# Second layer of groups 1 to 8 as seven half-size products, with fp16 sums of h and wo, and max terms on ScalarE

## The chip, the cores and the metric

The kernel runs on one core of one Trainium2 chip. The metric is the device time of one execution in microseconds (us); lower is better. Each time below is the median of the runs of one kernel, with the lowest and the highest beside it. A profiled execution is shown next to the times; its span is a little shorter than the device time (319.2 us of span for 321.17 us of device time in the kernel before).

## The reference

Linear attention with phi(x) = elu(x) + 1 on 8 batches, 8 heads, 576 positions and head size 64, followed by a SwiGLU feed-forward block on the 4608 tokens (d_model 512, d_ff 1536). Inputs and outputs are fp32.

```python
q_p, k_p = phi(q), phi(k)                       # phi(x) = max(x, 0) + min(exp(x), 1)
kv  = einsum('bhsd,bhse->bhde', k_p, v)
z   = sum(k_p, axis=2)
x   = einsum('bhsd,bhde->bhse', q_p, kv) / (einsum('bhsd,bhd->bhs', q_p, z)[..., None] + 1e-06)
x   = x.transpose(0, 2, 1, 3).reshape(4608, 512)
out = (silu(x @ w_gate) * (x @ w_val)) @ w_out  # 512 -> 1536 -> 512
```

## The kernel before

The kernel works in fp16 with fp32 accumulation. The 4608 tokens are nine groups g = 0 to 8 of 512. In each group, layer 1 has twelve blocks `fb`. A block is four gate matmuls and four value matmuls of 512 columns; ScalarE then applies silu, and VectorE multiplies it with the value half into `hT`. Layer 2 has four token tiles of twelve 512-column matmuls each, and one eviction per tile (times 1/SC) into `osb`, which goes out by DMA. While TensorE works on group g, the other engines prepare the attention of the next batches: phi of k and q, the denominators (`prod`, reduce, reciprocal, scale), a transpose by DMA, and on TensorE the small matmuls `mm2` (they give `xT`, the input of the next group) and `mm1` (k times v; called through `joint`).

```python
def phi(src, e, dst, b, lp):                     # e holds exp(src), from ScalarE
    s = slice(2 * lp, 2 * lp + 2)
    nc.vector.tensor_scalar(out=e[:, s, :], in0=e[:, s, :], scalar1=1.0, scalar2=None, op0=ALU.min)
    for l in range(2 * lp, 2 * lp + 2):
        nc.vector.scalar_tensor_tensor(              # max(src, 0) + e, 576 columns
            out=dst[b % 2][:, :, D * l:D * l + D],
            in0=src[b % 2][:, l, :].rearrange("p (j d) -> p j d", d=D), scalar=0.0,
            in1=e[:, l, :].rearrange("p (j d) -> p j d", d=D), op0=ALU.max, op1=ALU.add)

def l1_gate(g, fb):
    (pg, pv), s = l1_banks(g, fb), sil[fb % 2]
    nc.scalar.activation(out=s[:, :], in_=pg[:, :], func=AF.Silu, bias=0.0, scale=1.0)
    nc.vector.scalar_tensor_tensor(out=hT[g % 2][:, fb, :], in0=pv[:, :], scalar=SC, in1=s[:, :],
                                   op0=ALU.mult, op1=ALU.mult)

def l2(g, t, f0=0, f1=FB):
    pso[(g, t)] = (pV[0], pG[0], pV[1], pG[1])[t]
    for fb in range(f0, f1):
        nc.tensor.matmul(out=pso[(g, t)][:, :], lhsT=hT[g % 2][:, fb, P * t:P * t + P], rhs=wo[:, fb, :],
                         start=(fb == 0), stop=(fb == FB - 1))
# ... l2_out: one eviction of 512 columns, then two output transfers on SyncE's queue
# ... l2_last: the last tile of group 8 in two halves of 256 columns, its outputs on two queues

def prep(b):                                     # phi of batch b, slotted after the four tiles
    return at(4, [(0, lambda: exp_k(b, 0)), (0, lambda: exp_k(b, 1)), (1, lambda: exp_q(b, 0)),
                  (1, lambda: exp_q(b, 1)), (1, lambda: phi_k(b, 0)), (2, lambda: phi_k(b, 1)),
                  (3, lambda: nc.scalar.preload_act_table_set("silu_and_others")), (3, lambda: phi_q(b, 0))])

for g in range(1, NG):
    # ... sl: side work after each block; w: leftovers of it for layer 2 (in group 1: two denominator steps)
    for fb in range(FB):
        l1(g, fb)
        for f in sl[fb]:
            f()
        # ... loads of later batches, issued by GpSimd
    for t in range(4):
        if t == 3 and b1 < NG:
            mm2(b1, pV[2], "AVAV")
            if b2 < B:
                joint(b2)
        # ... l2_last for the last tile of the last group
        l2(g, t)
        for f in w[t] + pre[t]:
            f()
        l2_out(g, t, A if t in (1, 3) else V)
```

In these traces VectorE and ScalarE take their work in program order (below, VectorE stands idle for 1.19 us with later work ready, and silu on ScalarE starts only after max terms of 1.18 and 1.16 us), so where a call stands in this loop is where it stands in their queues.

## Time and profile before

| | before |
|---|---|
| time, median of 3 runs (lowest to highest) | 321.0 us (320.78 to 321.17) |
| span of the profiled run | 319.2 us |
| TensorE, VectorE, ScalarE, GpSimd busy | 98%, 66%, 54%, 10% |
| layer 2 of a steady group, from its first matmul to the next group's layer 1 | 11.66 us |
| layer 1 of a steady group | 20.93 us |
| from the modelled end of the last matmul to the end of the span | 4.6 us |

From the page of the kernel before: busy time and share of each engine with its instruction count, the granted TensorE clock over 40 equal slices in tenths, and the chain of work that ended last by engine.

```profile
PE 311.8 (98%) x2191; PEld 148.5 (47%) x2191; DVE 211.3 (66%) x393; ACT 171.3 (54%) x246; POOL 31.9 (10%) x47
...
PEclk9999999999999999999999999999999999999999
...
PE 89%; DMA 4%; DVE 2%; POOL 2%; ACT 2%; issue 1%; SPq 0%; POOLq 0%; ACTq 0%
```

TensorE (PE) is busy 98% of the span at a mean granted clock of 0.998, and the chain that ended last lies on it for 89%. So a microsecond of TensorE is a microsecond of the kernel, and other engines' time counts only where TensorE waits for it.

From the timeline of TensorE in the kernel before, in layer 2 of group 3. The columns are start, duration, engine, line, operation, output and inputs, shape and count.

```profile
142.69 2.75 PE L303 MATMUL pV<-wo,hT 128*128 128x512 f16 x12
145.28 2.75 PE L303 MATMUL pG<-wo,hT 128*128 128x512 f16 x12
```

From the same view, at the end of group 8:

```profile
311.79 1.47 PE L324 MATMUL pG<-wo,hT 128*128 128x256 f16 x12
313.10 1.47 PE L324 MATMUL pX<-wo,hT 128*128 128x256 f16 x12
```

The starts are 2.59 us apart for 12 matmuls of 512 columns, or 216 ns each, and 1.31 us for 12 of 256, or 109 ns each. The last tile of this kernel thus already shows the pace of the half-size products.

### The profile page before, as it was taken

How to read it: one execution, taken by the hardware profiler on the slowest of the kernel's cores; microseconds unless marked ns; L12 is line 12 of the kernel's file. 1: busy time of each engine (PE TensorE's matmuls, PEld its weight loads, DVE VectorE, ACT ScalarE, POOL GpSimd, SP SyncE). 2: the span in 40 equal slices, each digit the busy share in tenths (PEclk: the TensorE clock that was granted, in tenths of full speed). 3: DMA queues.
4: the chain of work that ended last, by engine and by line, in shares of the span. 5: the costliest groups of instructions: out<-in, count | busy, mean ns of one | idle time of the engine just before them, and what ended most of it. 6: DMA issues, size and time to landing. Idle time of an engine off the chain costs nothing.

```text
span 319.2 us, 5573 instructions
## 1 busy us (share of the span) xinstructions
PE 311.8 (98%) x2191; PEld 148.5 (47%) x2191; DVE 211.3 (66%) x393; ACT 171.3 (54%) x246; POOL 31.9 (10%) x47
## 2 busy tenths in 40 slices
PE   8999999999999999999999999999999999999994
PEld 6644453444444454445444454445444444444443
DVE  3747749878978877887888787877883344134411
ACT  3869969748563765467536754585431333133310
POOL 8535310010020001000010000000000000000000
PEclk9999999999999999999999999999999999999999
DMA  7999999994579147924792430233022400140014
GB/s 101 194 200 200 204 207 208 260 210 85 118 140 166 33 93 139 154 46 90 142 149 50 87 74 0 49 71 89 2 49 59 101 0 0 35 99 0 2 35 97
DMA packets 40986, 32.21 MB, mean 101 GB/s; under 512 B 16256, under 2 KB 36480, under 8 KB 40960
## 3 DMA queue, kind: packets, MB, share of 16 engines
q0 software_dynamic: 20640, 18.88, 38.0%
q1 hardware_dynamic: 20160, 12.85, 18.4%
q8 instruction: 17, 0.28, 0.4%
q10 hardware_dynamic: 160, 0.13, 0.2%
q14 instruction: 9, 0.07, 0.1%
HBM read 37.75 MB, written 9.44 MB: 148 GB/s over the span
## 4 chain that ended last, share of the span: by engine, by line
PE 89%; DMA 4%; DVE 2%; POOL 2%; ACT 2%; issue 1%; SPq 0%; POOLq 0%; ACTq 0%
PE pV L282 28%; PE pG L282 27%; PE pV L303 14%; PE pG L303 13%; DMA wv<-in_moe_w_val_dram 3%; PE pX L282 2%; PE pX L254 1%; DVE osb L313 1%; DMA out_dram<-osb 1%; PE pV L172 1%; DVE xT L435 1%; ACT rr L432 1%; ACT rr L429 1%; POOL k L99 0%; POOL v L99 0%
## 5 line engine op out<-in xcount | busy, mean ns | idle before, releaser
L288 DVE SCALAR_TENSOR_TENSOR hT<-pV,sil 128x512 f16<-128x512 f32 x105 | 72.2, 691 | 57.0 <-PE pV L282 53.2
L282 PE MATMUL pV<-xT,wv 128*128 128x512 f16 x420 | 108.1, 379 | 0.3 <-DMA wv<-in_moe_w_val_dram 0.3
L282 PE MATMUL pG<-xT,wg 128*128 128x512 f16 x408 | 105.1, 379 | 0.7 <-DVE osb L313 0.6
L287 ACT ACTIVATE sil<-pG 128x512 f16<-128x512 f32 x102 | 60.6, 597 | 78.4 <-PE pG L282 51.2
L282 PEld LDWEIGHTS <-wv 128*128 128x128 f16 x432 | 42.2, 98 | 51.6 <-DMA wv<-in_moe_w_val_dram 1.1
L282 PEld LDWEIGHTS <-wg 128*128 128x128 f16 x432 | 41.8, 98 | 51.0 <-issue 1.5
L303 PEld LDWEIGHTS <-hT 128*128 128x128 f16 x420 | 39.8, 98 | 47.6 <-issue 1.2
L303 PE MATMUL pV<-wo,hT 128*128 128x512 f16 x216 | 50.2, 379 | 0.0
L303 PE MATMUL pG<-wo,hT 128*128 128x512 f16 x204 | 47.6, 380 | 0.0
L313 DVE TENSOR_SCALAR osb<-pV 128x512 f32<-128x512 f32 x18 | 12.4, 690 | 25.3 <-PE pV L303 25.3
L311 ACT ACTIVATE osb<-pG 128x512 f32<-128x512 f32 x15 | 8.8, 589 | 19.9 <-PE pG L303 19.8
L127 DVE SCALAR_TENSOR_TENSOR kp<-k,ek 128x576 f16<-128x576 f16 x24 | 17.1, 755 | 0.4
L127 DVE SCALAR_TENSOR_TENSOR qp<-q,eq 128x576 f16<-128x576 f16 x24 | 17.1, 755 | 0.4
L235 DVE TENSOR_TENSOR qp<-qp,rden 128x768 f16<-128x768 f16 x18 | 17.1, 949 | 0.0
L222 DVE TENSOR_REDUCE den<-prod 128x12 f32<-128x768 f16 x18 | 17.0, 943 | 0.0
L269 ACT ACTIVATE xT<-pX 128x512 f16<-128x512 f32 (+1 forms) x14 | 7.4, 579 | 16.7 <-PE pX L254 9.3
L121 ACT ACTIVATE ek<-k 128x1152 f16<-128x1152 f16 x14 | 15.6, 1154 | 0.1
L121 ACT ACTIVATE eq<-q 128x1152 f16<-128x1152 f16 x14 | 15.4, 1148 | 0.0
L147 ACT ACTIVATE vm<-v 128x1152 f16<-128x1152 f16 x12 | 14.1, 1175 | 0.0
L96 POOL DMA_DIRECT2D k<-in_k_dram x7 | 5.4, 766 | 76.8 <-DVE kp L127 53.8
L365 PE MATMUL pX<-sil,ones 128*128 128x256 f16 x51 | 8.9, 350 | 1.3 <-DVE sil L356 1.3
L217 DVE TENSOR_TENSOR prod<-qp,zbc 128x768 f16<-128x768 f16 x18 | 9.3, 516 | 1.4 <-ACT zbc L208 1.3
(105 smaller groups left out, 218.1 us busy)
## 6 DMA issues: line engine op xcount, KB each, us to landing
out_dram<-osb SPq DMA_DIRECT2D x70, 128.0 KB, 2.4
k<-in_k_dram POOLq DMA_DIRECT2D x7, 576.0 KB, 13.2
q<-in_q_dram POOLq DMA_DIRECT2D x7, 576.0 KB, 7.5
v<-in_v_dram POOLq DMA_DIRECT2D x7, 576.0 KB, 9.6
wg<-in_moe_w_gate_dram POOLq DMA_DIRECT2D x6, 256.0 KB, 11.7
wv<-in_moe_w_val_dram POOLq DMA_DIRECT2D x6, 256.0 KB, 11.9
wo<-in_moe_w_out_dram POOLq DMA_DIRECT2D x3, 512.0 KB, 15.8
k<-in_k_dram POOLq DMA_DIRECT2D x2, 288.0 KB, 5.7
```

Source lines behind the costliest of these rows:

```text
L121: nc.scalar.activation(out=e[:, s, :], in_=src[b % 2][:, s, :], func=AF.Exp, bias=0.0, scale=1.0)
L127: nc.vector.scalar_tensor_tensor(out=dst[b % 2][:, :, D * l:D * l + D], in0=src[b % 2][:, l, :].rearrange("p (j d) -> p j d", d=D), scalar ...
L147: nc.scalar.activation(out=vm[b % 2][:, :, s, 0:D].rearrange("p j l d -> p l j d"), in_=v16[b % 2][:, s, :].rearrange("p l (j d) -> p l j ...
L217: nc.vector.tensor_tensor(out=prod[:, 0:j1 - j0, :], in0=qp[b % 2][:, j0:j1, :], in1=zbc[:, :].unsqueeze(1).to_broadcast([P, j1 - j0, HL * ...
L222: nc.vector.tensor_reduce(out=den[:, HL * j0:HL * j1], in_=prod[:, 0:j1 - j0, :].rearrange("p j (l d) -> p (j l) d", d=D), axis=AX.X, op=A ...
L235: nc.vector.tensor_tensor(out=qv, in0=qv, in1=rden[:, HL * j0:HL * j1].unsqueeze(2).to_broadcast([P, HL * (j1 - j0), D]), op=ALU.mult)
L282: nc.tensor.matmul(out=ps[:, :], lhsT=src[:, i, P * fb:P * fb + P], rhs=xT[i][g % 2][:, :], start=(i == 0), stop=(i == 3))
L287: nc.scalar.activation(out=s[:, :], in_=pg[:, :], func=AF.Silu, bias=0.0, scale=1.0)
L288: nc.vector.scalar_tensor_tensor(out=hT[g % 2][:, fb, :], in0=pv[:, :], scalar=SC, in1=s[:, :], op0=ALU.mult, op1=ALU.mult)
L303: nc.tensor.matmul(out=pso[(g, t)][:, :], lhsT=hT[g % 2][:, fb, P * t:P * t + P], rhs=wo[:, fb, :], start=(fb == 0), stop=(fb == FB - 1))
L313: nc.vector.tensor_scalar(out=o[:, :], in0=ps[:, :], scalar1=1.0 / SC, scalar2=None, op0=ALU.mult)
L365: nc.tensor.matmul(out=dst[:, 0:256], lhsT=ones[:, :], rhs=sil[0][:, 0:256], start=True, stop=True)
```

## The change

The intent is to do less on TensorE. Split h into two halves by token and two halves by d_ff (even and odd blocks), and wo into two halves by d_ff and two by column. The Winograd form of Strassen's scheme then needs seven products of half-size blocks in place of eight: 84 matmuls of 256 columns per group in place of 48 of 512. It needs four sums of the blocks of h in every group (on VectorE), four sums of the blocks of wo once (on GpSimd, in group 0), and combinations of the products. Most of the combinations are made by letting products accumulate in the same bank; ScalarE keeps copies of the partial results (`part`), and VectorE adds them in the eviction. To make room on VectorE, the max term of phi moves to ScalarE for batches 3 to 7. The diff, cut to its core (with the lambdas of `prep` and the index expressions shortened):

```diff
+def relu(src, dst, b, lp):                       # max(src, 0), 1152 columns
+    s = slice(2 * lp, 2 * lp + 2)
+    nc.scalar.activation(out=dst[b % 2][...], in_=src[b % 2][...], func=AF.Relu, bias=0.0, scale=1.0)
+def phi_sum(e, dst, b, lp):
+    nc.vector.tensor_scalar(out=e[:, s, :], in0=e[:, s, :], scalar1=1.0, scalar2=None, op0=ALU.min)
+    nc.vector.tensor_tensor(out=d, in0=d, in1=e[:, s, :]..., op=ALU.add)
 def phi_k(b, lp):
-    phi(k16, ek, kp, b, lp)
+    phi_sum(ek, kp, b, lp) if b > 2 else phi(k16, ek, kp, b, lp)
 # ... phi_q likewise

+def h_sum(g, m, f0, f1):                         # four sums or differences of blocks of hT
+    nc.vector.tensor_tensor(out=hs[:, m, f0:f1, :], in0=a, in1=b, op=op)
+def w_sum(m, f0, f1):                            # four differences of blocks of wo
+    nc.gpsimd.tensor_tensor(out=ws[:, m, f0:f1, :], in0=a, in1=b, op=ALU.subtract)
+def prd(g, n, tt):                               # product n for token half-tile tt: 6 matmuls of 256
+    for f in range(HF):
+        nc.tensor.matmul(out=(z if n in (2, 3, 5) else x)[:, 0:HD], lhsT=left(f), rhs=right(f),
+                         start=(f == 0 and n in (1, 2, 5)), stop=(f == HF - 1), ...)
+def keep(tt, i, from_x):                         # ScalarE: partial result to SBUF
+    nc.scalar.activation(out=part[:, 2 * i + tt, :], in_=(x if from_x else z)[:, 0:HD], func=AF.Copy, ...)
+def fin(tt, th, ch, i, from_x):                  # VectorE: bank * 1/SC + part -> osb
+    nc.vector.scalar_tensor_tensor(out=osb[...], in0=..., scalar=1.0 / SC, in1=part[:, 2 * i + tt, :], ...)
+def put(g, tt, th, c0=0, c1=DM, engs=(nc.sync, nc.sync)):
+    # ... two output transfers
+def l2_steps(g):
+    return [(p[1][0],), (p[1][1], k1[0]), (p[2][0], k1[1]), (p[2][1], c11[0]), (p[6][0], c11[1]), (p[6][1], k2[0]),
+            (p[5][0], k2[1]), (p[5][1], k5[0]), (p[7][0], k5[1]), (p[7][1], c22[0]), (p[3][0], c22[1]),
+            (p[3][1], lambda: c12(0)), (p[4][0], lambda: c12(1)), (p[4][1], lambda: fin_21(g, 0)),
+            (lambda: fin_21(g, 1),)]

 def prep(b):
-    return at(4, [(0, exp_k(b, 0)), (0, exp_k(b, 1)), (1, exp_q(b, 0)), (1, exp_q(b, 1)), (1, phi_k(b, 0)),
-                  (2, phi_k(b, 1)), (3, preload of silu), (3, phi_q(b, 0))])
+    return at(16, [(2, exp_k(b, 0)), (6, exp_k(b, 1)), (6, phi_k(b, 0)), (8, phi_k(b, 1)), (9, exp_q(b, 0)),
+                   (10, exp_q(b, 1)), (14, preload of silu), (14, phi_q(b, 0))])

 # group 0, layer 2, before each third of it:
+        for m in range(4):
+            w_sum(m, 2 * i, 2 * i + 2)
 # groups 1 to 8:
+            for lp in range(2):
+                sl[4 + lp].append(lambda lp=lp: relu_k(b2, lp))
+                sl[6 + lp].append(lambda lp=lp: relu_q(b2, lp))
+        for m in range(4):
+            sl[(8, 8, 9, 10)[m]].append(lambda m=m: h_sum(g, m, 0, 4))
+            sl[11].append(lambda m=m: h_sum(g, m, 4, 6))
+        for t in range(3):
+            pre[3 * t + 2][:0] = w[t]            # leftovers of the denominator
+        for (i, step) in enumerate(l2_steps(g)):
+            for f in step: f()
+            if i == (11 if g == 1 else 8) and b1 < NG:
+                mm2(b1, (pV[1], pG[1], pV[0], pG[0]), "AVAV")
+            if i == (9 if g == 1 else 10) and b2 < B:
+                joint(b2)
+            for f in pre[i]: f()
```

Products are numbered as in the code. Products 1 and 2 read `hT` itself, 5, 6 and 7 read a sum of h and a sum of wo, 3 reads a sum of h, and 4 a sum of wo. Product 5 starts in the bank that product 2 used, so it waits for the first eviction.

More of the change, by code (lines that the diff above doesn't have):

```diff
@@ L74 @@
     osb = two([P, DM], FP32, "osb", 4)
+    hs = sb.tile([P, 4, FB // 2, U * C // 2], FP16, name="hs")
+    ws = sb.tile([P, 4, FB // 2, DM // 2], FP16, name="ws")
+    part = sb.tile([P, 6, DM // 2], FP32, name="part")
     wg = sb.tile([P, 4, DF], FP16, name="wg")
@@ L84 @@
     pX = [pp.tile([P, 512], FP32, name=f"pX_{i}") for i in range(3)]
-    turn = [0]
-    def bank():
-        turn[0] += 1
-        return pX[turn[0] % 3]
     def heads(src, b):
@@ L130, in phi, with relu_k, relu_q @@
                 in1=e[:, l, :].rearrange("p (j d) -> p j d", d=D), op0=ALU.max, op1=ALU.add)
+    def relu(src, dst, b, lp):
+        s = slice(2 * lp, 2 * lp + 2)
+        nc.scalar.activation(out=dst[b % 2][:, :, P * lp:P * lp + P].rearrange("p j (s d) -> p s j d", d=D),
+                             in_=src[b % 2][:, s, :].rearrange("p s (j d) -> p s j d", d=D),
+                             func=AF.Relu, bias=0.0, scale=1.0)
+    def relu_k(b, lp):
+        relu(k16, kp, b, lp)
+    def relu_q(b, lp):
+        relu(q16, qp, b, lp)
+    def phi_sum(e, dst, b, lp):
+        s = slice(2 * lp, 2 * lp + 2)
+        nc.vector.tensor_scalar(out=e[:, s, :], in0=e[:, s, :], scalar1=1.0, scalar2=None, op0=ALU.min)
+        d = dst[b % 2][:, :, P * lp:P * lp + P].rearrange("p j (s d) -> p s j d", d=D)
+        nc.vector.tensor_tensor(out=d, in0=d, in1=e[:, s, :].rearrange("p s (j d) -> p s j d", d=D), op=ALU.add)
     def exp_k(b, lp):
@@ L138, in phi_k @@
     def phi_k(b, lp):
-        phi(k16, ek, kp, b, lp)
+        phi_sum(ek, kp, b, lp) if b > 2 else phi(k16, ek, kp, b, lp)
     def phi_q(b, lp):
-        phi(q16, eq, qp, b, lp)
+        phi_sum(eq, qp, b, lp) if b > 2 else phi(q16, eq, qp, b, lp)
     def vcast(b, lp):
@@ L159, in mm1 @@
         if lp == 0:
-            kvb[b] = ((pV[2], pX[0]), (pX[2], pV[2]), (pX[0], pX[1]), (pV[0], pG[0]))[min(b, 3)]
+            kvb[b] = ((pV[2], pX[0]), (pX[2], pV[2]), (pX[0], pX[1]), (pV[1], pG[1]))[min(b, 3)]
         for j in range(J):
@@ L200, in zb @@
     def zb(b):
-        zps[b] = bank()
+        zps[b] = pX[0]
         nc.tensor.matmul(out=zps[b][:, :], lhsT=ones[:, :], rhs=zd[:, :, :].rearrange("p i c -> p (i c)"),
@@ L255, in corners, with mm2 @@
                                      rhs=qT[b % 2][rows, j0:j1, lp, C * hh:C * hh + C], start=True, stop=True)
-    def mm2(g, spare, engs):
-        ps = [bank(), bank(), bank(), spare]
+    def mm2(g, ps, engs):
         us = units(g)
@@ L317, in l2_out @@
                               in_=o[C * e:C * e + C, :])
-    def l2_last(g, t):
-        banks = (pG[1], pX[0])
-        for h in range(2):
-            for fb in range(FB):
-                nc.tensor.matmul(out=banks[h][:, 0:256], lhsT=hT[g % 2][:, fb, P * t:P * t + P],
-                                 rhs=wo[:, fb, 256 * h:256 * h + 256], start=(fb == 0), stop=(fb == FB - 1))
-        for h in range(2):
-            for e in range(2):
-                o = osb[ot[0] % 4]
-                ot[0] += 1
-                rows = slice(C * e, C * e + C)
-                if e == 0:
-                    nc.vector.tensor_scalar(out=o[rows, 0:256], in0=banks[h][rows, 0:256], scalar1=1.0 / SC,
-                                            scalar2=None, op0=ALU.mult)
-                else:
-                    nc.scalar.activation(out=o[rows, 0:256], in_=banks[h][rows, 0:256], func=AF.Copy, bias=0.0,
-                                         scale=1.0 / SC)
-                b, j = units(g)[2 * t + e]
-                (nc.sync, nc.scalar)[e].dma_start(
-                    out=out[S * b:S * b + S, 256 * h:256 * h + 256].rearrange("(c j) f -> j c f", j=J)[j],
-                    in_=o[rows, 0:256])
@@ new lines, with h_blk, w_blk @@
+    HF, HT, HD = FB // 2, U * C // 2, DM // 2
+    def h_blk(g, kh, th, f0, f1):
+        return hT[g % 2][:, 2 * f0 + kh:2 * f1 - 1 + kh:2, HT * th:HT * th + HT]
+    def w_blk(kh, ch, f0, f1):
+        return wo[:, 2 * f0 + kh:2 * f1 - 1 + kh:2, HD * ch:HD * ch + HD]
+    def h_sum(g, m, f0, f1):
+        o = hs[:, m, f0:f1, :]
+        (a, b, op) = ((h_blk(g, 0, 1, f0, f1), h_blk(g, 1, 1, f0, f1), ALU.add),
+                      (hs[:, 0, f0:f1, :], h_blk(g, 0, 0, f0, f1), ALU.subtract),
+                      (h_blk(g, 0, 0, f0, f1), h_blk(g, 0, 1, f0, f1), ALU.subtract),
+                      (h_blk(g, 1, 0, f0, f1), hs[:, 1, f0:f1, :], ALU.subtract))[m]
+        nc.vector.tensor_tensor(out=o, in0=a, in1=b, op=op)
@@ new lines, in w_sum, with l2_banks, left, right @@
+    def w_sum(m, f0, f1):
+        o = ws[:, m, f0:f1, :]
+        (a, b) = ((w_blk(0, 1, f0, f1), w_blk(0, 0, f0, f1)), (w_blk(1, 1, f0, f1), ws[:, 0, f0:f1, :]),
+                  (w_blk(1, 1, f0, f1), w_blk(0, 1, f0, f1)), (w_blk(1, 0, f0, f1), ws[:, 1, f0:f1, :]))[m]
+        nc.gpsimd.tensor_tensor(out=o, in0=a, in1=b, op=ALU.subtract)
+    def l2_banks(tt):
+        return (pX[0], pX[1])[tt], (pX[2], pV[2])[tt]
+    def prd(g, n, tt):
+        (x, z) = l2_banks(tt)
+        th = P * tt
+        def left(f):
+            h = hT[g % 2]
+            return {1: h[:, 2 * f, th:th + P], 2: h[:, 2 * f + 1, th:th + P], 3: hs[:, 3, f, th:th + P],
+                    4: h[:, 2 * f + 1, HT + th:HT + th + P], 5: hs[:, 0, f, th:th + P], 6: hs[:, 1, f, th:th + P],
+                    7: hs[:, 2, f, th:th + P]}[n]
+        def right(f):
+            return {1: wo[:, 2 * f, 0:HD], 2: wo[:, 2 * f + 1, 0:HD], 3: wo[:, 2 * f + 1, HD:DM], 4: ws[:, 3, f, :],
+                    5: ws[:, 0, f, :], 6: ws[:, 1, f, :], 7: ws[:, 2, f, :]}[n]
+        for f in range(HF):
+            nc.tensor.matmul(out=(z if n in (2, 3, 5) else x)[:, 0:HD], lhsT=left(f), rhs=right(f),
+                             start=(f == 0 and n in (1, 2, 5)), stop=(f == HF - 1), skip_group_check=True)
@@ new lines, in keep @@
+    def keep(tt, i, from_x):
+        (x, z) = l2_banks(tt)
+        nc.scalar.activation(out=part[:, 2 * i + tt, :], in_=(x if from_x else z)[:, 0:HD], func=AF.Copy, bias=0.0,
+                             scale=1.0 / SC)
+    def fin(tt, th, ch, i, from_x):
+        (x, z) = l2_banks(tt)
+        nc.vector.scalar_tensor_tensor(out=osb[2 * th + tt][:, HD * ch:HD * ch + HD],
+                                       in0=(x if from_x else z)[:, 0:HD], scalar=1.0 / SC, in1=part[:, 2 * i + tt, :],
+                                       op0=ALU.mult, op1=ALU.add)
@@ new lines, in put, with fin_21 @@
+    def put(g, tt, th, c0=0, c1=DM, engs=(nc.sync, nc.sync)):
+        for e in range(2):
+            b, j = units(g)[2 * (2 * th + tt) + e]
+            engs[e].dma_start(out=out[S * b:S * b + S, c0:c1].rearrange("(c j) f -> j c f", j=J)[j],
+                              in_=osb[2 * th + tt][C * e:C * e + C, c0:c1])
+    def fin_21(g, tt):
+        x = l2_banks(tt)[0]
+        o = osb[2 + tt]
+        if g < NG - 1 or tt == 0:
+            nc.scalar.activation(out=o[:, 0:HD], in_=x[:, 0:HD], func=AF.Copy, bias=0.0, scale=1.0 / SC)
+            put(g, tt, 1)
+            return
+        put(g, tt, 1, HD, DM)
+        nc.vector.tensor_scalar(out=o[0:C, 0:HD], in0=x[0:C, 0:HD], scalar1=1.0 / SC, scalar2=None, op0=ALU.mult)
+        nc.scalar.activation(out=o[C:P, 0:HD], in_=x[C:P, 0:HD], func=AF.Copy, bias=0.0, scale=1.0 / SC)
+        put(g, tt, 1, 0, HD, (nc.sync, nc.scalar))
@@ new lines, in l2_steps, with c12 @@
+    def l2_steps(g):
+        p = [[(lambda n=n, tt=tt: prd(g, n, tt)) for tt in range(2)] for n in range(8)]
+        k1, k2, k5 = [[(lambda i=i, tt=tt, x=x: keep(tt, i, x)) for tt in range(2)]
+                      for (i, x) in ((0, True), (1, True), (2, False))]
+        c11 = [lambda tt=tt: fin(tt, 0, 0, 0, False) for tt in range(2)]
+        c22 = [lambda tt=tt: fin(tt, 1, 1, 2, True) for tt in range(2)]
+        def c12(tt):
+            fin(tt, 0, 1, 1, False)
+            put(g, tt, 0)
+        return [(p[1][0],), (p[1][1], k1[0]), (p[2][0], k1[1]), (p[2][1], c11[0]), (p[6][0], c11[1]), (p[6][1], k2[0]),
+                (p[5][0], k2[1]), (p[5][1], k5[0]), (p[7][0], k5[1]), (p[7][1], c22[0]), (p[3][0], c22[1]),
+                (p[3][1], lambda: c12(0)), (p[4][0], lambda: c12(1)), (p[4][1], lambda: fin_21(g, 0)),
+                (lambda: fin_21(g, 1),)]
@@ L601, in prep @@
     def prep(b):
-        return at(4, [(0, lambda: exp_k(b, 0)), (0, lambda: exp_k(b, 1)), (1, lambda: exp_q(b, 0)),
-                      (1, lambda: exp_q(b, 1)), (1, lambda: phi_k(b, 0)), (2, lambda: phi_k(b, 1)),
-                      (3, lambda: nc.scalar.preload_act_table_set("silu_and_others")), (3, lambda: phi_q(b, 0))])
+        return at(16, [(2, lambda: exp_k(b, 0)), (6, lambda: exp_k(b, 1)), (6, lambda: phi_k(b, 0)),
+                       (8, lambda: phi_k(b, 1)), (9, lambda: exp_q(b, 0)), (10, lambda: exp_q(b, 1)),
+                       (14, lambda: nc.scalar.preload_act_table_set("silu_and_others")), (14, lambda: phi_q(b, 0))])
     def ld_b(b):
@@ L657 @@
         sl, w = [[] for _ in range(FB)], [[] for _ in range(4)]
-        pre = [[] for _ in range(4)]
+        pre = [[] for _ in range(16)]
         if b1 < B:
@@ L662 @@
             pre = prep(b2)
-            sl[8].append(lambda: vcast(b2, 0))
-            sl[9].append(lambda: vcast(b2, 1))
+            for lp in range(2):
+                sl[4 + lp].append(lambda lp=lp: relu_k(b2, lp))
+                sl[6 + lp].append(lambda lp=lp: relu_q(b2, lp))
+                sl[8 + lp].append(lambda lp=lp: vcast(b2, lp))
+        for m in range(4):
+            sl[(8, 8, 9, 10)[m]].append(lambda m=m: h_sum(g, m, 0, 4))
+            sl[11].append(lambda m=m: h_sum(g, m, 4, 6))
         for fb in range(FB):
@@ L672 @@
                 ld_b(3)
-        for t in range(4):
-            if t == 3 and b1 < NG:
-                mm2(b1, pV[2], "AVAV")
-                if b2 < B:
-                    joint(b2)
-            if g == NG - 1 and t == 3:
-                l2_last(g, t)
-                continue
-            l2(g, t)
-            for f in w[t] + pre[t]:
-                f()
-            l2_out(g, t, A if t in (1, 3) else V)
+        for t in range(3):
+            pre[3 * t + 2][:0] = w[t]
+        for (i, step) in enumerate(l2_steps(g)):
+            for f in step:
+                f()
+            if i == (11 if g == 1 else 8) and b1 < NG:
+                mm2(b1, (pV[1], pG[1], pV[0], pG[0]), "AVAV")
+            if i == (9 if g == 1 else 10) and b2 < B:
+                joint(b2)
+            for f in pre[i]:
+                f()
 _INS = ['q', 'k', 'v', 'moe_w_gate', 'moe_w_val', 'moe_w_out']
```

## The prediction

> **What bounds it.** The engine table gives TensorE 98% of the 319.2 us span, VectorE 66%, ScalarE 54%; the chain of waits lies 89% on TensorE. The timeline shows 512-column matmuls 216 ns apart (12 in 2.59 us) at full clock. A steady group takes 32.6 us: 20.7 layer 1, 10.4 layer 2 (48 matmuls), the rest attention matmuls.
>
> **Removed.** In eight groups, 48 matmuls of 512 columns become 84 of 256. The last tile of before already runs such ones: 12 in 1.31 us, 109 ns each. So 84 x 0.109 = 9.2 us against 10.4: 1.2 us per group, 9.5 us in all, all on the critical path. The ceiling is about 311 us.
>
> **Added (estimates from trace durations, per group).**
> - VectorE: eight sums of h. An fp16 two-input op of 768 elements takes 0.50 us, of 1152 0.76 us; so about 0.65 us for 1024, 0.38 us for 512: 4 us. Six 256-wide evictions (0.42 us) for two 512-wide (0.69 us): +1.1. Each phi: 0.76 us for two of 0.755: -3.0.
> - ScalarE: four max terms (like the 1.17 us cast of v), six partial copies (about 0.38 us), two output copies: +6 us on about 20 of 32. It fits.
> - GpSimd: 12 sums of wo in group 0.
>
> **Where the gain is lost.** VectorE has room on average but works in order:
> 1. The h sums come at blocks 8 to 11 of layer 1, where VectorE idled 0.17 us per 1.73 us block. I get a lag of 1.1 us at the last hT. Product 2 waits 0.3 us, product 6 0.3 us for its sums, product 5 0.1 us for the first eviction.
> 2. mm2 now comes after product 7; its two xT evictions (1.2 us) precede the second phi of k (1.2 us) on VectorE, which the k-v matmuls need. TensorE has only 1.3 us of products in between: about 1.0 us lost, groups 2 to 5.
> 3. In group 1 the leftover reduce, reciprocal and scale (2.2 us) precede the first eviction, on which product 5 waits: over 2, altogether about 3.5 us lost.
> 4. The wo sums precede the loads of batch 3 in GpSimd's queue (issued at 37 to 45 us now), delaying these by over 10 us, to near where ScalarE needs k in group 1. [...]
>
> Sum: groups 7 and 8 gain 1.2 us each, group 6 about 0.5; groups 2 to 5 roughly break even; group 1 loses about 2; group 0 loses 0 to 2; the tail gains up to 0.9. I lean to a small gain, since such estimates of waits tend to be too high.
>
> **Predicted: 319.5 us, range 315.5 to 325. Chances: faster by over 2% 0.12, within 2% 0.82, slower 0.06.**
>
> **What would show it.** Right: products 109 ns apart; layer 2 of groups 7 and 8 shrinks by 1.2 us; TensorE idles on VectorE at product 5 in group 1 and at the k-v matmuls in groups 2 to 5; VectorE above 70%. Wrong: no TensorE idle in those groups (then about 312 us), or waits on ScalarE.
>
> **What would make it wrong.** Faster h sums or phi: 312 to 315. A starved ScalarE in group 1, or a costly fight of GpSimd with VectorE: over 325.

GpSimd's sums of wo might hold up VectorE in group 0, by "one or two us", and no trace showed the reason. The sum still has that term, as "group 0 loses 0 to 2": it was the author's estimate without a trace. The terms of the sum (2.9 us gained in groups 6 to 8 and up to 0.9 at the tail, about 2 lost in group 1 and 0 to 2 in group 0) came to a time of about 319 to 322 us, of which 319.5 was predicted.

## More of the kernel before

From the timeline of VectorE in the kernel before, in layer 2 of group 0 (the phi of a k that is computed beside it) and in group 1.

```profile
49.82 1.43 DVE L127 SCALAR_TENSOR_TENSOR kp<-k,ek 128x576 f16<-128x576 f16 x2
51.35 0.62 DVE L435 SCALAR_TENSOR_TENSOR xT<-pX,rr 128x448 f16<-128x448 f32 x1
...
52.42 0.68 DVE L313 TENSOR_SCALAR osb<-pV 128x512 f32<-128x512 f32 x1
53.02 0.45 DVE L125 TENSOR_SCALAR ek<-ek 128x1152 f16<-128x1152 f16 x1
...
80.79 0.96 DVE L235 TENSOR_TENSOR qp<-qp,rden 128x768 f16<-128x768 f16 x1
81.67 0.68 DVE L313 TENSOR_SCALAR osb<-pV 128x512 f32<-128x512 f32 x1
```

Two phi pieces of 576 columns take 1.43 us here. In group 1 the last denominator steps, which are left over from layer 1 (the scale at 80.79 is the last of them), come just before the first eviction of layer 2 at 81.67. In this kernel nothing on TensorE waits for that eviction.

## The result and the profile after

| | before | after |
|---|---|---|
| time, median of 4 runs (lowest to highest) | 321.06 us (320.78 to 321.17) | 331.19 us (329.93 to 331.95) |
| span of the profiled run | 319.2 us | 330.2 us |
| TensorE, VectorE, ScalarE busy | 98%, 66%, 54% | 93%, 71%, 62% |

The ratio is 1.031, with a 95% interval of 1.029 to 1.034: the change is slower by 3%. Ratios here are the mean time of one kernel's fast runs over that of the other's of the same rounds, so they are not quite the ratio of the quoted medians.

From the page of the kernel after, the same parts as before.

```profile
PE 308.5 (93%) x2467; PEld 173.7 (53%) x2467; DVE 235.8 (71%) x468; ACT 205.1 (62%) x313; POOL 46.3 (14%) x59
...
PEclk9999999999989999999999999999999999999997
...
PE 63%; DVE 23%; issue 4%; DMA 3%; ACT 3%; POOL 2%; DVEq 0%; POOLq 0%; ACTq 0%
```

TensorE has less busy work, but its share of the chain fell from 89% to 63%, and VectorE (DVE) took 23% of it. In one slice within the work the granted clock fell to 0.8 (the 7 in the last slice comes after the last matmul). TensorE is no longer the only thing that counts.

The stages, from the first matmul of one to the first matmul of the next on the timeline of TensorE (the last row but one to the modelled end of the last matmuls), in us:

| stage | before | after | difference | best case, from 84 x 109 ns for 48 x 216 ns |
|---|---|---|---|---|
| layer 2 of group 0 | 16.49 | 18.45 | +1.96 | 0 |
| layer 1 of group 1 | 22.01 | 22.16 | +0.15 | 0 |
| layer 2 of group 1 | 11.56 | 17.46 | +5.90 | -1.2 |
| layer 2 of groups 2 to 5, mean | 11.67 | 12.40 | +0.72 each | -1.2 each |
| layer 2 of group 6 | 11.03 | 10.74 | -0.29 | -1.2 |
| layer 2 of group 7 | 11.02 | 9.84 | -1.18 | -1.2 |
| layer 2 of group 8 | 10.55 | 9.33 | -1.22 | -1.2 |
| after the last matmul | 4.6 | 6.9 | +2.3 | 0 |

Layer 1 of groups 2 to 8 takes 20.93 or 20.72 us in both. The differences sum to +10.5; the start of layer 2 of group 0 adds 0.5, which makes the 11.0 us between the spans. (That start is not part of the change: over the twelve profiles of kernels that start alike it lay between 38.6 and 39.6 us, and once at 40.8. So stages are compared below, not spans.) Where nothing waits, in groups 7 and 8, the whole expected gain is there. The rest was lost in four places. (Group 6 has the waits for hT and the sums, as groups 2 to 5, but no k-v matmuls.)

**Groups 2 to 5.** From the timeline of TensorE in the kernel after, layer 2 of group 2 (in brackets is the idle time just before, and what ended it).

```profile
118.59 2.46 PE L373 MATMUL pX<-wo,hT 128*128 128x256 f16 x18
120.89 0.82 PE L373 MATMUL pV<-wo,hT 128*128 128x256 f16 x6
...
122.43 1.82 PE L373 MATMUL pX<-ws,hs 128*128 128x256 f16 x14 [0.28 <-DVE hs L347]
...
128.56 0.22 PE L187 MATMUL pV<-vm,kp 64*64 64x65 f16 x2 [0.62 <-DVE kp L145]
```

The first eighteen matmuls take 2.30 us to the next start, where they take 1.97 in group 7 (283.37 to 285.34): the difference is the wait for the last `hT`. The sums of h show 0.28 us of idle time (the eighteen matmuls with them, from 121.54 on, take 2.54 us to the next start, against 1.96 in group 8). The long one is in the k-v matmuls: those of the first half are done by about 127.9, and those of the second half wait for `kp` until 128.56. The timeline of VectorE in the kernel after shows why.

```profile
124.10 0.76 DVE L145 TENSOR_TENSOR kp<-kp,ek 128x1152 f16<-128x1152 f16 x1
126.05 1.29 DVE L285 TENSOR_SCALAR xT<-pG 128x512 f16<-128x512 f32 x2 [1.19 <-PE pG L269]
127.26 0.45 DVE L143 TENSOR_SCALAR ek<-ek 128x1152 f16<-128x1152 f16 x1
127.74 0.76 DVE L145 TENSOR_TENSOR kp<-kp,ek 128x1152 f16<-128x1152 f16 x1
```

VectorE finishes the first half of phi(k) before 124.9, then stands idle for 1.19 us until the attention matmuls feed the eviction to `xT`, and only after that takes up the second half of phi(k) (127.26 and 127.74), for which TensorE is waiting. All its inputs were there (the exponential of this half ended at 124.95 us on ScalarE's timeline). It stood behind `xT` only because of its place in the queue.

**Group 1.** From the timeline of TensorE in the kernel after, layer 2 of group 1.

```profile
81.95 1.48 PE L373 MATMUL pX<-wo,hT 128*128 128x256 f16 x12 [1.04 <-DVE hT L302]
83.90 0.28 PE L373 MATMUL pX<-wo,hT 128*128 128x256 f16 x1 [0.46 <-DVE hT L302]
...
85.56 1.05 PE L373 MATMUL pX<-ws,hs 128*128 128x256 f16 x8 [0.29 <-DVE hs L347]
88.89 0.81 PE L373 MATMUL pX<-ws,hs 128*128 128x256 f16 x6 [2.28 <-DVE osb L383]
...
90.23 2.77 PE L373 MATMUL pX<-ws,hs 128*128 128x256 f16 x12
```

There are waits of 1.04 and 0.46 us for `hT`, of 0.29 for the sums, and of 2.28 us at product 5 for the first eviction, and then a batch of 12 matmuls takes 2.77 us where the batch at 81.95 takes 1.48. The granted clock was 0.51 there. From the activity by stretches of the kernel after, its own columns being the stretch, its length, busy time and count of PE, PEld, DVE, ACT and POOL, then the granted clock, the DMA share and GB/s.

```profile
86.80:88.80 2.00, 0.00 (x0) 0.00 (x0) 1.90 (x6) 1.28 (x2) 0.00 (x0) 1.00 0.06 11
90.20:93.60 3.40, 3.40 (x66) 2.35 (x67) 1.68 (x4) 0.38 (x1) 0.00 (x0) 0.51 0.97 134
```

From the timeline of VectorE in the kernel after, group 1: three multiplications into hT of layer 1, then what comes before the first eviction of layer 2.

```profile
69.30 0.69 DVE L302 SCALAR_TENSOR_TENSOR hT<-pV,sil 128x512 f16<-128x512 f32 x1 [1.03 <-ACT sil L301]
70.83 0.69 DVE L302 SCALAR_TENSOR_TENSOR hT<-pV,sil 128x512 f16<-128x512 f32 x1 [0.84 <-ACT sil L301]
...
73.28 0.69 DVE L302 SCALAR_TENSOR_TENSOR hT<-pV,sil 128x512 f16<-128x512 f32 x1 [1.25 <-ACT sil L301]
...
87.54 0.96 DVE L250 TENSOR_TENSOR qp<-qp,rden 128x768 f16<-128x768 f16 x1
88.42 0.42 DVE L383 SCALAR_TENSOR_TENSOR osb<-pX,part 128x256 f32<-128x256 f32 x1
```

VectorE waits for ScalarE's silu (`sil`), 1.03, 0.84 and 1.25 us. The first of these waits has another cause (copies of the k-v result stand ahead of that silu, and g1_late below has the same 1.03 us). Before the other two, ScalarE worked on the max terms (1.18 us at 69.14 and 1.16 us at 71.46 on its timeline), behind which silu stood in its queue. Later the last steps of the denominator (the scale at 87.54) stand ahead of the first eviction (88.42), as they did before. But now product 5 waits for it.

**Group 0.** From the timeline of VectorE in the kernel after, the phi of k beside layer 2 of group 0.

```profile
50.26 2.39 DVE L124 SCALAR_TENSOR_TENSOR kp<-k,ek 128x576 f16<-128x576 f16 x2
52.57 0.61 DVE L515 SCALAR_TENSOR_TENSOR xT<-pX,rr 128x448 f16<-128x448 f32 x1
...
53.63 0.68 DVE L327 TENSOR_SCALAR osb<-pV 128x512 f32<-128x512 f32 x1
54.23 0.86 DVE L122 TENSOR_SCALAR ek<-ek 128x1152 f16<-128x1152 f16 x1
55.13 2.26 DVE L124 SCALAR_TENSOR_TENSOR kp<-k,ek 128x576 f16<-128x576 f16 x2
```

From the timeline of GpSimd (POOL) in the kernel after.

```profile
52.11 1.55 POOL L353 TENSOR_TENSOR ws<-wo,ws 128x512 f16<-128x512 f16 x1
53.63 1.15 POOL L353 TENSOR_TENSOR ws<-wo 128x512 f16<-128x512 f16 x1
```

Two phi pieces, which took 1.43 us, take 2.39 and 2.26 us while GpSimd works on the sums of wo; the minimum took 0.86 instead of 0.45. The operations with an input in PSUM (`xT` at 52.57 and `osb` at 53.63) take 0.61 and 0.68 us, against 0.62 and 0.68 before. GpSimd's sums take longer too: 1.15 us each up to 48.41 us on this timeline, and 1.74 and 1.55 for those at 50.29 and 52.11, beside the first two phi pieces.

**The tail.** From the timeline of SyncE's transfer queue (SPq) in the kernel before, at its end.

```profile
307.53 6.29 SPq L316 DMA_DIRECT2D out_dram<-osb  x6
313.91 1.67 SPq L338 DMA_DIRECT2D out_dram<-osb  x2
```

From the same view of the kernel after:

```profile
321.78 5.78 SPq L390 DMA_DIRECT2D out_dram<-osb  x9
```

Before, most of the output of the last group had been issued while TensorE was still at work. After, nine transfers go through one queue one after the other, 5.78 us for nine or about 0.64 us each, the greater part of it after the last matmul's end at about 323.3 us.

### The profile page after: what moved, and what is told of

The parts are those of the page before. It is cut to its first block, busy times and chain, and to the rows that moved or that the text cites. A ratio compares the mean times of both kernels' runs of the same rounds, so it can differ in the third digit from the quotient of the medians.

```text
span 330.2 us, 6314 instructions
## 1 busy us (share of the span) xinstructions
PE 308.5 (93%) x2467; PEld 173.7 (53%) x2467; DVE 235.8 (71%) x468; ACT 205.1 (62%) x313; POOL 46.3 (14%) x59
## 4 chain that ended last, share of the span: by engine, by line
PE 63%; DVE 23%; issue 4%; DMA 3%; ACT 3%; POOL 2%; DVEq 0%; POOLq 0%; ACTq 0%
PE pV L296 21%; PE pG L296 20%; PE pX L373 12%; DVE hs L347 5%; DVE hT L302 5%; PE pV L373 4%; DMA wv<-in_moe_w_val_dram 3%; DVE qp L250 3%; PE pX L296 2%; DVE den L237 2%; DVE xT L285 2%; PE pV L269 1%; DVE kp L145 1%; DVE xT L515 1%; DVE kp L124 1%
## 5 line engine op out<-in xcount | busy, mean ns | idle before, releaser
L373 PEld LDWEIGHTS <-hs 128*128 128x128 f16 x384 | 36.8, 99 | 12.3 <-DVE hs L347 3.4
L373 PE MATMUL pX<-ws,hs 128*128 128x256 f16 x240 | 32.9, 280 | 4.0 <-DVE osb L383 2.3
L373 PEld LDWEIGHTS <-hT 128*128 128x128 f16 x288 | 27.1, 98 | 9.7 <-DVE hT L302 4.7
L378 ACT ACTIVATE part<-pX 128x256 f32<-128x256 f32 x40 | 15.3, 381 | 20.8 <-PE pX L373 20.4
L373 PE MATMUL pX<-wo,hT 128*128 128x256 f16 x144 | 19.0, 273 | 1.5 <-DVE hT L302 1.5
L347 DVE TENSOR_TENSOR hs<-hT 128x1024 f16<-128x1024 f16 (+1 forms) x32 | 17.6, 550 | 0.1
L285 DVE TENSOR_SCALAR xT<-pG 128x512 f16<-128x512 f32 (+1 forms) x14 | 8.7, 666 | 10.9 <-PE pG L269 10.9
L118 ACT ACTIVATE eq<-q 128x1152 f16<-128x1152 f16 x14 | 15.9, 1157 | 0.0
L383 DVE SCALAR_TENSOR_TENSOR osb<-pX,part 128x256 f32<-128x256 f32 x32 | 12.6, 416 | 3.6 <-PE pX L373 3.6
L373 PE MATMUL pX<-ws,hT 128*128 128x256 f16 x96 | 11.8, 273 | 0.0
L131 ACT ACTIVATE kp<-k 128x1152 f16<-128x1152 f16 x10 | 11.6, 1157 | 0.0
```

Of the source, the lines that this page charges most:

```text
L118: nc.scalar.activation(out=e[:, s, :], in_=src[b % 2][:, s, :], func=AF.Exp, bias=0.0, scale=1.0)
L285: nc.vector.tensor_scalar(out=dst, in0=ps[i][:, c00:], scalar1=1.0 / SC, scalar2=None, op0=ALU.mult)
L347: nc.vector.tensor_tensor(out=o, in0=a, in1=b, op=op)
L373: nc.tensor.matmul(out=(z if n in (2, 3, 5) else x)[:, 0:HD], lhsT=left(f), rhs=right(f), start=(f == 0 and n in (1, 2, 5)), stop=(f == HF ...
L378: nc.scalar.activation(out=part[:, 2 * i + tt, :], in_=(x if from_x else z)[:, 0:HD], func=AF.Copy, bias=0.0, scale=1.0 / SC)
L383: nc.vector.scalar_tensor_tensor(out=osb[2 * th + tt][:, HD * ch:HD * ch + HD], in0=(x if from_x else z)[:, 0:HD], scalar=1.0 / SC, in1=pa ...
```

## The experiments

The theory after reading the two traces: the loss comes from orders within queues. On VectorE they are the second half of phi(k) behind `xT`, and the leftovers ahead of the first eviction in group 1; on SyncE it is one queue for all last outputs; and in group 0 it is GpSimd keeping VectorE from its work. The rivals were: that the late loads of batch 3 (now issued by GpSimd at 56 to 58 us, behind the sums of wo) starve group 1; that the max terms on ScalarE are the cost; and that the amount of VectorE work, not its order, is. Each kernel is the changed one with one edit, unless said otherwise.

### kphi_early: second half of phi(k) ahead of xT

```diff
-   (8, lambda: phi_k(b, 1)),      # after mm2 and its evictions to xT
+   (7, lambda: phi_k(b, 1)),
```

> The changed kernel with one edit: the second phi of k goes one step earlier, ahead of mm2's evictions. Theory (the order of VectorE's work makes TensorE wait): VectorE sits idle 1.2 us before the xT evictions in groups 2 to 5 and has the exponential it needs by then, so it fills that idle time; the 1.3 us wait at the k-v matmuls goes and layer 2 of groups 2 to 5 falls from 12.4 to about 11.3 us each, 4 to 5 us in all: about 327 us. Rival (VectorE has too much work per group, whatever the order): the wait only moves on to the evictions of mm2 or the next layer 1, and the time stays within 1 us of 331.

Measured: 328.30 us (327.63 to 329.84), before 320.70; ratio 1.024 (1.021 to 1.028). From the timeline of VectorE in kphi_early, group 2.

```profile
125.16 0.76 DVE L145 TENSOR_TENSOR kp<-kp,ek 128x1152 f16<-128x1152 f16 x1
125.84 1.28 DVE L285 TENSOR_SCALAR xT<-pG 128x512 f16<-128x512 f32 x2
```

The second half of phi(k) now fills the time in which VectorE had stood idle, and `xT` starts only 0.1 us later in its stage (7.56 us after the stage's start instead of 7.46). Layer 2 of groups 2 to 5 went from 12.36 to 12.44 us down to 11.55 to 11.57, by 0.83 us each. The order was the cost there. What remains of the difference from the best case is for the most part the waits for hT and for the sums. (The stage was forecast at about 11.3 us and the time at 327; both came out a little higher.)

### g1_old: group 1 alone with the old second layer

```diff
+   if g == 1:                      # 48 matmuls of 512, the old slots of phi, no sums of h
+       ... l2(g, t), w[t] + prep_old(b2)[t], l2_out(g, t, ...)
+       continue
```

> The changed kernel, but group 1 has its second layer the old way (no h sums, no products); groups 2 to 8 and the max terms as in the change. Theory: group 1's layer 2 goes back from 17.5 to about 11.6 us, the granted clock never falls to 0.5, and the time is about 325 us. Rival (group 1 is long because ScalarE is behind with the max terms of batch 3, which stay here): layer 2 of group 1 stays above 13.5 us and the time above 327.

Measured: 327.05 us (326.60 to 327.43); ratio 1.019 (1.017 to 1.021). Layer 2 of group 1 went from 17.46 to 11.68 us, but layer 1 of that group took 23.32 instead of 22.16: in this profile the clock was at 0.50 for the first 2.9 us of it. So the forecast that the clock never falls to 0.5 failed, and the time stayed 2 us above the forecast 325; the interval of the ratio includes 1.02. Group 1 is the costliest place, and the change gains nothing there. The remaining groups of this variant stayed as in the change.

### tail_two: outputs of the last group on two queues

```diff
-def put(..., engs=(nc.sync, nc.sync)):
+    engs = engs or ((nc.sync, nc.scalar) if g == NG - 1 else (nc.sync, nc.sync))
```

> The changed kernel, but the last group's output transfers are issued from two queues in turn. Theory: the 9 issues of 0.6 us each in one queue make the last transfer late; from the last matmul to the end falls from 6.9 us to 5 or less, time about 329 us. Rival (the transfers themselves are slow because they bunch up): the end moves by less than 0.5 us.

Measured: 328.62 us (328.01 to 329.54); ratio 1.024 (1.022 to 1.027). The time from the last matmul to the end fell from 6.9 to 5.4 us, by 1.5 (the forecast was 5 or less). The rest of the better median is something else. In the profile of this kernel there is no stretch at half clock, and layer 2 of group 1, whose code is the same, takes 15.90 us instead of 17.46. So this run happens to tell what the half clock costs: 1.56 us, in the runs that have it. (kphi_early and fill, without such a stretch, also take 15.9 us there.) The mean clock over a run fits: the three runs of the change at 0.988 to 0.991 took 331.08 to 331.95 us, and the one at 0.997 took 329.93.

### no_wsum: no sums of wo (wrong result)

```diff
-       for m in range(4):
-           w_sum(m, 2 * i, 2 * i + 2)
+   nc.gpsimd.memset(ws, 0)          # at the start, so that something is there to read
```

> Wrong result on purpose: the 12 sums of wo on GpSimd are not made, ws stays zero. Theory ([...] VectorE's phi of batch 2 takes 1.2 instead of 0.75 us per piece): the gap of 2.6 us before layer 1 of group 1 falls to about 0.6, and the time to about 329 us, and the phi pieces in group 0 take 0.75 us again. Rival (the delayed loads of batch 3 are what costs): the phi pieces stay at 1.2 us. [...]

(The theory is that GpSimd's sums lengthen VectorE's phi pieces.)

Measured: 333.11 us (332.98 to 333.33); ratio 1.038; the result is wrong, as it has to be. The forecast of 329 us was missed, and the time as a whole says nothing: the memset delayed the loads behind it in GpSimd's queue, and layer 2 of group 0 started at 42.50 us instead of 39.59. The stage does: layer 2 of group 0 took 16.48 us instead of 18.45, as in the kernel before (16.49), and the two phi pieces took 1.43 us again. So the sums on GpSimd cost group 0 its 1.96 us. In this kernel the loads of batch 3 were no longer held up by the sums, and layer 2 of group 1 was no shorter for it (17.56 us). The rival of late loads falls.

### max_only and no_max: the two halves of the change apart

`max_only` is the kernel before plus the max terms on ScalarE alone. `no_max` is the change without them.

```diff
# no_max
-   phi_sum(ek, kp, b, lp) if b > 2 else phi(k16, ek, kp, b, lp)
+   phi(k16, ek, kp, b, lp)
-               sl[4 + lp].append(lambda lp=lp: relu_k(b2, lp))
-               sl[6 + lp].append(lambda lp=lp: relu_q(b2, lp))
```

> The kernel before with the second half of the change alone: max terms of batches 3 to 7 on ScalarE, phi on VectorE as min and sum; second layer as before. Theory (TensorE bounds the kernel before, both engines have room): the time stays within 0.5% of 321, VectorE's busy time falls by about 12 us and ScalarE's rises by about 23. Rival (the max terms make the gate's activations late): the layer 1 stages grow beyond 20.9 us and the time rises by 1% or more.

> The changed kernel without its second half: products and h sums as in the change, but phi wholly on VectorE (two scalar-tensor-tensor pieces of 0.75 us in place of one sum of 0.76). Theory: VectorE's queue sets the pace of layer 2 in groups 2 to 5, and each phi of k before the k-v matmuls is 0.7 us longer, so layer 2 grows from 12.4 to 13.5 us or more in each of these groups and the time to 335 or more. Rival (ScalarE's extra work is what costs): faster than 331.

Measured for max_only: 320.91 us (320.74 to 321.17), before 320.73; ratio 1.000 (0.999 to 1.002), and all stages as in the kernel before; VectorE's busy time fell by 13.1 us and ScalarE's rose by 20.7. Measured for no_max: 334.75 us (333.14 to 335.27); ratio 1.043 (1.040 to 1.046); layer 2 of groups 2 to 5 took 13.03 to 13.11 us instead of 12.36 to 12.44. By themselves the max terms change nothing, because in the kernel before TensorE does not wait for VectorE or ScalarE after layer 1 of group 1 has started (its list of waits has none from there on); inside the change they save about 0.67 us in each of groups 2 to 5. As the cost they are ruled out for those groups. For group 1 they are not: see g1_late.

### g1_left: the leftovers of group 1 after the first evictions

```diff
-   pre[3 * t + 2][:0] = w[t]
+   pre[4 if g == 1 else 3 * t + 2][:0] = w[t]
```

> The changed kernel, but in group 1 the leftover reduce, reciprocal and scale stand after the first evictions instead of before them. Theory (VectorE's amount of work ahead of the k-v matmuls is what counts in group 1): product 5 no longer waits its 2.3 us, but the k-v matmuls then wait about as long for the second phi of k; layer 2 of group 1 stays within 1 us of 15.9 (the value with the clock at full). Rival (only that order is at fault): it falls to about 13.6 us.

Measured: 330.12 us (329.58 to 330.76); ratio 1.029 (1.026 to 1.031); layer 2 of group 1 took 15.54 us, against 15.90 without the half clock for the change. The wait at product 5 is gone (the list of waits has none), but waits of the k-v matmuls for `kp` took its place. From the list of waits in this stretch of g1_left (who waited for what, total, times, longest), limited to group 1's layer 2.

```profile
PEld L187 <- DVE kp L145: 2.1, 2, 1.3
...
PE pV L187 <- DVE kp L145: 1.7, 2, 1.0
```

The first line is the weight loads of the k-v matmuls and the second the matmuls themselves, so the same two waits are seen twice; the matmuls lost 1.7 us. In group 1 there is no idle time on VectorE to move the work into (it is busy for 1.90 of the 2.00 us from 86.80 in the kernel after), as there is in groups 2 to 5. There the amount, not the order, decides, so the third rival holds for this group.

### g1_late: max terms of group 1 two blocks later

```diff
-   sl[4 + lp].append(relu_k); sl[6 + lp].append(relu_q); sl[8 + lp].append(vcast)
+   d = 2 if g == 1 else 0           # relu_k at 6 + lp, relu_q at 8 + lp, vcast at 10 + lp
```

> The changed kernel, but in group 1 alone the max terms of batch 3 and the cast of its v come two blocks later (blocks 6 to 11 instead of 4 to 9), after the gate activations of blocks 4 and 5, which are late because of the copies of R. Theory (ScalarE's max terms keep the gate activations late from block 4 on, so VectorE enters the h sums already 1.1 us behind, which my forecast left out): VectorE is on time at block 8, the last hT of group 1 ends about 1 us earlier, the waits at products 1 and 2 shrink from 1.5 to about 0.4 us together, and layer 2 of group 1 falls from 15.9 (at full clock) to about 15. Rival (it is VectorE's own work in blocks 4 to 7 that makes it late): layer 2 of group 1 stays at 15.9, apart from a stretch at half clock.

Measured: 331.16 us (329.40 to 331.99); ratio 1.031 (1.027 to 1.035), so no gain in time. The step in the middle was right: VectorE was no longer late in the late blocks. The last hT ended 2.58 us after layer 1 did, instead of 3.64; the wait of 1.04 us in product 1 was gone; product 5 started 7.63 us after the end of layer 1 instead of 8.69. Layer 2 of group 1 went from 17.46 to 16.50 us, in two profiles that both have a stretch at half clock. So the lag that ScalarE passes on to VectorE is worth about 1 us. This edit also moved the cast of v, but no_max, which leaves the cast where it was and has no max terms, shows the same: only the first of the three waits for silu is left, product 5 starts 7.64 us after the end of layer 1, and layer 2 of group 1 takes 16.48 us, with a stretch at half clock in it. So it is the max terms. The device time does not show it: one stretch at half clock more or less, worth 1.56 us, is larger, and the runs of both kernels scatter by 2 us or more. Only the stages show this gain.

### fill: useless matmuls in the gaps of group 1

The question was if the half clock follows from the waits. 20 matmuls of 256 columns, whose results nobody reads, are put ahead of layer 1 of group 1 and ahead of product 5.

```diff
+   if g == 1: warm(20, pX[1])       # before layer 1
+   if g == 1 and i == 6: warm(20, pG[0])
```

> The changed kernel plus 40 matmuls of 256 columns with no use, 20 at the wait before layer 1 of group 1 and 20 before product 5 of group 1, into banks that are free there; each 20 take 2.2 us at full clock, as long as the waits that they fill. Theory (the granted clock falls to 0.5 for 3.4 us after such a wait): no stretch at half clock is left, layer 2 of group 1 takes about 16 us and its layer 1 22.2, and the median falls by up to 1.5 us below 331 although TensorE does more work. Rival (the half clock comes from something else, or comes at random): a stretch at 0.5 still shows, or the time grows by up to 4 us.

Measured: 329.73 us (329.55 to 330.50, five runs); ratio 1.028 (1.027 to 1.030), against 1.031 (1.029 to 1.034) for the change. From the activity by stretches of fill, around the same place.

```profile
91.00:93.00 2.00, 2.00 (x77) 1.61 (x68) 1.42 (x6) 0.77 (x3) 0.00 (x0) 1.00 1.20 196
```

The clock was 1.00 in this stretch and in the three of 2 us before it, and layer 2 of group 1 took 15.90 us although TensorE was given more to do. The five runs lie within 1 us, where those of the change lie within 2.

The result fits the theory that the half clock follows from such waits. What brings it on in one profile and not in another was not shown. In the kernel after, the wait of 2.60 us before layer 1 of group 1 was followed by a clock of 1.00, and the shorter one of 2.28 us at product 5 by the 0.51 shown above. In tail_two, where the code of group 1 is the same, the wait at product 5 was 2.28 us too, and no half clock followed. So the length of the wait alone does not tell the two apart.

### best1 and best2: putting the findings together

`best1` is the change with phi_k(b, 1) at step 7, exp_q(b, 1) at step 9, two queues at the end, group 1 as before, two of the four sums of h moved into layer 2 (steps 4 and 6), and the sums of wo on GpSimd in group 1. `best2` moves the sums of wo to VectorE (two thirds in group 0, where it idles for 2.71 us in the kernel after, the rest at block 4 of group 1), and gives the first two evictions to `xT` to ScalarE.

```diff
# best2, besides the edits of kphi_early, tail_two and g1_old
-   nc.gpsimd.tensor_tensor(out=ws[...], in0=a, in1=b, op=ALU.subtract)
+   nc.vector.tensor_tensor(out=ws[...], in0=a, in1=b, op=ALU.subtract)
+   pre[4].append(lambda: h_sum(g, 2, 0, 6))
+   pre[6].append(lambda: h_sum(g, 3, 0, 6))
-   mm2(b1, (pV[1], pG[1], pV[0], pG[0]), "AVAV")
+   mm2(b1, (pV[1], pG[1], pV[0], pG[0]), "AAVV")
```

> All repairs together: group 1's layer 2 the old way; the second phi of k before mm2's evictions; h sums 2 and 3 made in layer 2 behind the first evictions, so that the last hT is not late; the second exponential of q before the copies of R; the sums of wo on GpSimd after the loads of batch 4, during group 1; the last group's transfers in two queues. Theory: layer 2 of groups 2 to 5 falls to about 10.4 to 10.7 us, of group 6 to 10, group 0 back to 16.5; about 314 us. Rival (VectorE has too much work whatever the order, or GpSimd's sums cost as much in group 1 as in group 0): 318 or more.

> As best1, but the sums of wo are made on VectorE: those of the first two thirds of wo in group 0, where it idles about 2.7 us after the copies of R, the rest at block 4 of group 1; and mm2's four evictions are two on ScalarE, then two on VectorE, so that the banks of the k-v matmuls come free earlier. Theory: no contention is left; layer 2 of group 1 returns from 15.6 to about 11.7 us, that of groups 2 to 5 falls from 11.0 to about 10.5; about 314 us. Rival (VectorE has no room left in groups 0 and 1): group 1 stays above 13 us and the time above 316.

Measured for best1: 320.10 us (319.28 to 321.96); ratio 0.999 (0.995 to 1.002). Layer 2 of groups 2 to 5 fell to 11.01 us and of group 0 to 16.42 us, but layer 2 of group 1, in its old form, took 15.55 us: GpSimd's sums now slowed the denominators there (a product of 768 columns that takes 0.5 us took 1.3), so the transposes and with them the attention matmuls came late. In g1_old, with the same old form and no such sums in group 1, the stage took 11.68 us. The contention had moved with the sums, the forecast of 314 us was missed, and its rival came true.

Measured for best2: 314.23 us (313.80 to 314.71), before 320.91; ratio 0.980 (0.978 to 0.981); correct. From the page of best2, and below it from its timeline of TensorE, layer 2 of group 3.

```profile
PE 303.3 (97%) x2431; PEld 170.9 (55%) x2431; DVE 232.0 (74%) x450; ACT 203.1 (65%) x307; POOL 32.2 (10%) x47
...
PE 89%; DMA 3%; DVE 2%; ACT 2%; POOL 2%; issue 1%; ACTq 0%; POOLq 0%
```

From the timeline:

```profile
141.92 2.13 PE L373 MATMUL pX<-wo,hT 128*128 128x256 f16 x18
...
144.54 2.13 PE L373 MATMUL pX<-ws,hs 128*128 128x256 f16 x18
```

The chain is on TensorE for 89% again, and the two batches of eighteen take 2.13 us with no wait in them. Layer 2 of groups 2 to 5 takes 10.65 us, of group 6 9.84, of group 7 9.83, of group 8 9.32, of group 1 11.55 and of group 0 16.49; the tail is 5.4. This beats both kernels. It is what the change is worth with its costs taken away: about 1.0 to 1.2 us in each of seven groups, less 0.8 us at the end. As the edits of best2 were made together, the runs do not say what each of the last ones is worth alone.

## Why the prediction was right or wrong

The prediction was wrong in the size and the direction: 319.5 us and a range up to 325 were predicted, 331.19 was measured. The mechanisms it named were nearly all there; the sums were wrong. Three steps failed: the waits of group 1 (3.5 us forecast, 7.1 measured, with the half clock and silu's place behind the max terms left out), the addition for groups 2 to 5 ("roughly break even", measured +0.72 us each), and the sign of the tail (a gain of up to 0.9 us, measured a loss of 2.3).

- **Pace of the products: right.** 84 matmuls at 109 ns; groups 7 and 8 gained 1.18 and 1.22 us, for 1.2 predicted. Group 6 gained 0.29, for about 0.5.
- **Groups 2 to 5: right waits, wrong sum.** The list in the prediction gives 0.3 + 0.3 + 0.1 + 1.0 = 1.7 us lost against 1.2 gained, a loss of 0.5 us per group. The text then wrote "groups 2 to 5 roughly break even". The trace shows +0.72 us in each, 2.9 in all. The step that failed here is this addition, and with it the sentence "I lean to a small gain, since such estimates of waits tend to be too high". The waits were slightly too low, if anything; kphi_early confirmed the largest by taking 0.83 us per group away.
- **Group 1: right waits, mis-sized.** "Altogether about 3.5 us lost" was 7.1 in the profiled run: layer 2 took 17.46 us, where the steady stage without waits would take about 10.4 (11.56 less 1.2). Of this, 1.56 is the half clock (tail_two against the change), and about 1 of the remaining 5.5 is the lag that the max terms cause through ScalarE (1.06 at product 5 in g1_late, 1.05 in no_max). With both taken off, 4.5 us are left, one more than predicted. The waits listed in the trace (1.04, 0.46, 0.29 and 2.28 us, and 0.43 at the start of the next group) make 4.5 of the 5.5; the rest is small gaps that I did not itemize. The prediction looked at ScalarE only as a sum of busy time ("It fits") and not as a queue in which silu stands behind the max terms.
- **Group 0: right.** "Loses 0 to 2" was +1.96, at the upper end. The fight of VectorE and GpSimd was real: phi pieces with two SBUF inputs went from 0.715 to 1.19 us each and took 0.715 again in no_wsum, while operations with one input in PSUM took 0.61 and 0.68. How the two engines hold one another up, these traces do not show.
- **Late loads of batch 3: the delay was real, the harm was not.** They were issued at 56 to 58 us, and nothing in group 1 waited for them that the traces show; no_wsum, in which the sums did not hold them up, had the same group 1.
- **The tail: wrong sign.** "The tail gains up to 0.9" was +2.3. No token tile is complete before product 3 or 4, the last two, so nearly all outputs of the last group fall due in the last microseconds, through one queue. Two queues gave back 1.5 us. Part of this is how `put` is placed: VectorE evicts the first halves of two tiles already at 316.4 to 317.2 us in the kernel after, but they go out with their second halves, from 321.78 on. Sending them early was not tried.
- **VectorE above 70%, no waits on ScalarE as a cause of the steady groups: right.** VectorE was busy 71%.

Side by side, the terms of the sum that were off are: groups 2 to 5 by 2.9 us, group 1 by about 4 (+5.9 against "loses about 2"), the tail by 2.3 to 3.2, group 0 by about 1 from its middle. That is 10 to 11 us, and the miss is 11.7 us (331.19 against 319.5). It can't be reconciled more closely: the text was shaded by about a microsecond from its own items, the start of the profiled run was 0.5 us later, and the half clock differs from run to run.

What stays open: the last microsecond of group 1's loss, which no listed wait explains; what brings the half clock on, which followed a wait of 2.28 us in one profile and not in another; and what each of best2's last edits is worth alone.

## What to carry to other kernels

When a change takes work off the engine that bounds the kernel and puts more on the others, add up the waits group by group and believe the sum; then walk through each queue in its order and ask what stands in front of every instruction that the bounding engine waits for, ScalarE's and the transfer queues included. A share of busy time of 66% or 54% says that there is room, but not where in the queue it is: here moving one phi by a step took 0.83 us from each of four groups, and moving the constant sums off GpSimd took 1.96 us from one. And a split that spreads each output over several products completes whole rows of outputs only near the end, so the last group's transfers must be planned with it.
